# A new static order of instructions, and a new division of three kinds of work among the engines, in an attention and two-MLP kernel

## The chip, the cores and the metric

The kernel runs on one core of a Trainium2 chip. The metric is the device time of one execution, in microseconds (us), less is better. A core has a matrix engine (PE), a vector engine (DVE), an activation engine (ACT), a general engine (POOL) and a queue that issues the DMAs (SP). Each engine takes its instructions strictly in the order in which the program lists them, and waits where an instruction needs something that another engine has not finished. So the order of each list is a part of the program, and it is this order that the change makes anew.

## The reference, cut to what matters

Attention (2 batches, 8 heads, 768 positions, head size 64; a query sees 8 global keys and 96 local ones), then a first MLP with a rational activation, then a second one with a softmax gate and a layer norm.

```python
a = np.exp(scores - max); a = a / (sum + 1e-9); x = a @ v       # attention, masked
h = x @ w_in                                                     # 1536 x 512 @ 512 x 2048
P = a[0] + a[1]*h + a[2]*h**2 + a[3]*h**3
Q = 1.0 + abs(b[0])*abs(h) + abs(b[1])*h**2
g = P / (Q + 1e-6)
x = g @ w_out                                                    # 1536 x 2048 @ 2048 x 512
h = x @ w_in2; sm = softmax(h); solu = h * sm
ln = (solu - mu) / sqrt(var + 1e-6) * g_ln
out = ln @ w_out2
```

## The kernel before

**Words.** Matmul operands are kept as two words: a high one, which the matrix engine's rounded 32-bit type can hold, and a low one, the rest. Each product is three matmul passes: high by high, high by low, low by high. The weights come in as 64-bit numbers, and DVE makes 32-bit ones of each 128x512 piece in three steps (L705, L709, L713), 48 times; a copy then makes the high word (on the engine that the string WHX names) and a subtraction the low word (`minus`, L149, on POOL, or on DVE for the pieces listed in WDVE).

**Stages.** Tokens go in four blocks of 384. For a block, 12 attention units (one token tile of 128 by one pair of heads) fill x: scores on PE (L568, L571), masked maximum on DVE (L577), exponential on ACT (L585), transposes on PE (L601), their copy out by ACT or DVE (L619, chosen by TRX), the product with v on PE (L608, L614). After four units a tile is normalized on DVE (L637), transposed (L641) and split in two words. Then come the steps of the first MLP, 64 in all: block 0 with the first 8 of the 16 pieces of the hidden size, blocks 1, 2 and 3 with all 16, block 0 with the last 8 (its x was stored and is loaded again). A step is: 12 matmuls for h (L797, L799 for the high word of x, L803 for the low one); an elementwise chain for g; 9 matmuls of g with w_out (L890, L891, and L896 for the low word of g). From about 403 us on, a second phase handles the second MLP in 12 token tiles; there PE has nearly all the work (L977 to L979, L1062 to L1064).

**The elementwise chain of a step** reads h from a PSUM bank: two activations (ACT, L826 and L828), a product (DVE, L829), a square (DVE as L836 or ACT as L832, chosen by the string SQX, one letter a step), logarithm and exponential (ACT, L840, L841), three products (DVE: L842, L844, L846). L846 is the last; its result is g. EPX chooses where the chain's middle value lives: an SBUF tile ("t") or a PSUM bank. Then the high word of g is a copy (ACT, DVE or POOL, by GHX), and the low word is a subtraction, in the kernel before always on POOL (L149).

**What sets the order.** The program first records some 2,100 operations, each with its engine, a duration in a model and what it needs. A list scheduler (class `Plan`) then walks through model time and writes each engine's list: among the operations that can start, it takes the one whose due time, less a lead by kind (LEADS), is earliest. UW, WS and M2 say at which step the attention units of later blocks, the second half of the first MLP's weights, and the weights of the second MLP are recorded. Where the plan has a gap on PE of over 0.7 us, it puts small matmuls of the identity there (L389, "fill"). DVE instructions marked `lock` are those whose operands all lie in SBUF; the plan lets them wait for a POOL instruction that runs, and the other way round. SP's list holds all loads in the order of the plan. Nothing is decided while the kernel runs.

Of the kernel before, what the change touches and what calls it, by code (L numbers as in the profile page):

```python
# [35 lines left out]
UW = {1: (1, 4), 2: (8, 15), 3: (25, 9)}  # L36
# [9 lines left out]
WLEAD = 33.8  # L46
# [147 lines left out]
class Plan:  # L194
# [5 lines left out]
    SEM, PORT, PORT2 = 0.04, 0.02, 0.05  # L200
# [7 lines left out]
    def op(self, eng, lat, fn, r=(), w=(), new=(), occ=None, lock=False, lead=0.0, move=0.0, after=(), tag=""):  # L208
        o = Op()
        o.i, o.eng, o.lat, o.fn, o.lock, o.lead, o.move, o.tag = len(self.ops), eng, lat, fn, lock, lead + LEADS.get(tag, 0.0), move, tag  # L210
        o.occ = occ if occ is not None else lat - 0.1 if eng in ("ACT", "DVE") else lat
        if lock:
            o.lat, o.occ = o.lat + WAIT, o.occ + WAIT
# [44 lines left out]
    def late(self, d, o):  # L258
        return self.SEM + (0.05 if o.eng == "POOL" else 0.0) + (0.1 if d.eng == "POOL" and o.eng == "PE" else 0.0)
# [15 lines left out]
    def run(self, emit=True, fill=None):  # L275
# [14 lines left out]
        def add(o):  # L290
            o.t0 = max((d.end + self.late(d, o) for d in o.deps if d.eng != o.eng or o.eng in ("SP", "X")), default=0.0)
            ready[o.eng].append(o)
# [5 lines left out]
        while left:  # L298
# [53 lines left out]
            if o.lock:  # L352
                port = o.end - (self.PORT2 if e == "POOL" else self.PORT)
# [1078 lines left out]
```

## Time and profile before

| | us |
|---|---|
| median of 3 executions (lowest, highest) | 551.47 (551.41, 552.12) |
| the profiled execution | 551.61 |
| its span, first to last instruction | 549.8 |
| PE busy in the span | 525.0 (95%) |
| DVE busy | 469.3 (85%) |
| ACT busy | 319.9 (58%) |
| POOL busy | 138.3 (25%) |

The span and the profiled execution differ by 1.8 us, which lie outside the first and last instruction. Busy time of PE is from a record's start to its modelled end, and matmuls overlap: two that follow each other closely both count as running. How much work PE has is therefore read from the distance between the starts of matmuls in a stretch without a wait.

### The profile page before, as it was taken

To read this page: it belongs to the slowest core of one execution; us is meant where nothing else is said; L and a number is where in the kernel's file an instruction comes from. 1 tells how busy PE (TensorE), PEld (TensorE's weight loads), DVE (VectorE), ACT (ScalarE), POOL (GpSimd) and SP (SyncE) were. 2 spreads that over 40 slices of the span, in tenths; PEclk is the share of its full clock that TensorE was granted. 3 is DMA by queue.
4 is the path that set the end of the run, shared out by engine and by line. 5 is a ranking of instruction groups with operands and counts; after the bars stand their busy time and mean duration, and the time that the engine had idled before them with its cause. 6 is when DMAs were issued, how large, how long until landed. Compare 5 with 4: busy or idle time off the path is not lost.

```text
span 549.8 us, 9337 instructions
## 1 busy us (share of the span) xinstructions
PE 525.0 (95%) x3224; PEld 434.3 (79%) x3224; DVE 469.3 (85%) x1046; ACT 319.9 (58%) x733; POOL 138.3 (25%) x144
## 2 busy tenths in 40 slices
PE   7899897999999999999999999998999999999995
PEld 5577676887787877778988789887778888888885
DVE  6867898999999999879889999999978988788760
ACT  6559485987786765765868545547234443344330
POOL 1301142342441322113235435344530000000000
PEclk9899898999999999999999999999999999999998
DMA  7688664356446323530024511024166688747601
GB/s 239 182 265 312 178 207 126 112 156 202 147 156 203 111 67 101 179 135 1 0 78 138 202 62 40 4 93 153 39 221 222 222 272 262 255 163 257 232 38 44
DMA packets 34326, 83.53 MB, mean 152 GB/s; under 512 B 4192, under 2 KB 11616, under 8 KB 34272
## 3 DMA queue, kind: packets, MB, share of 16 engines
q1 hardware_dynamic: 34272, 82.86, 46.6%
q8 instruction: 27, 0.44, 0.3%
q14 instruction: 27, 0.22, 0.1%
HBM read 74.98 MB, written 7.86 MB: 151 GB/s over the span
## 4 chain that ended last, share of the span: by engine, by line
PE 56%; DVE 30%; ACT 9%; issue 3%; DMA 0%; ACTq 0%; DVEq 0%
PE pb L1062 4%; PE pb L1064 4%; DVE t L842 4%; PE pb L1063 4%; PE pb L979 4%; PE pb L977 4%; PE pb L978 4%; PE pb L797 4%; PE pb L614 4%; PE pb L799 4%; PE pb L803 3%; DVE t L846 3%; DVE t L836 3%; DVE pb L844 3%; DVE cv L709 3%
## 5 line engine op out<-in xcount | busy, mean ns | idle before, releaser
L149 POOL TENSOR_TENSOR g<-t,g 128x384 fp32r<-128x384 f32 x64 | 71.2, 1114 | 139.8 <-PE pb L896 47.0
L797 PE MATMUL pb<-x,w 128*128 128x384 f32 x256 | 89.6, 350 | 3.1 <-DVE t L829 2.4
L799 PE MATMUL pb<-x,w 128*128 128x384 f32 x256 | 87.4, 342 | 0.0
L890 PE MATMUL pb<-w,g 128*128 128x512 f32 x192 | 77.7, 405 | 1.8 <-DVE y L920 1.8
L891 PE MATMUL pb<-w,g 128*128 128x512 f32 x192 | 75.5, 393 | 0.0
L149 POOL TENSOR_TENSOR w<-wst,w 128x512 fp32r<-128x512 f32 x31 | 41.7, 1347 | 79.0 <-ACT w L669 42.7
L803 PE MATMUL pb<-x,w 128*128 128x384 f32 x256 | 57.9, 348 | 0.0
L826 ACT ACTIVATE t<-pb,poly 128x384 f32<-128x384 f32 x64 | 42.8, 668 | 25.1 <-PE pb L803 16.2
L896 PE MATMUL pb<-w,g 128*128 128x512 f32 x192 | 56.8, 404 | 0.0
L797 PEld LDWEIGHTS pb<-x,w 128*128 128x128 f32 x256 | 48.8, 191 | 8.4 <-DVE t L829 5.7
L799 PEld LDWEIGHTS pb<-x,w 128*128 128x128 f32 x256 | 48.9, 191 | 1.5
L585 ACT ACTIVATE e<-e,st 128x192 f32<-128x192 f32 (+1 forms) x96 | 41.9, 439 | 13.9 <-DVE st L577 13.7
L803 PEld LDWEIGHTS pb<-x,w 128*128 128x128 f32 x256 | 45.2, 190 | 5.4 <-issue 1.7
L890 PEld LDWEIGHTS pb<-w,g 128*128 128x128 f32 x192 | 36.0, 188 | 10.6 <-DVE y L920 2.7
L713 DVE SCALAR_TENSOR_TENSOR wst<-wst,cv 128x512 int32<-128x512 int32 x48 | 41.6, 868 | 1.0
L829 DVE SCALAR_TENSOR_TENSOR t<-t,poly,pb 128x384 f32<-128x384 f32 x64 | 38.7, 606 | 3.8 <-ACT t L828 3.4
L828 ACT ACTIVATE t<-pb,poly 128x384 f32<-128x384 f32 x64 | 36.9, 577 | 7.8 <-DVE t L844 4.4
L891 PEld LDWEIGHTS pb<-w,g 128*128 128x128 f32 x192 | 36.1, 188 | 5.8
L709 DVE SCALAR_TENSOR_TENSOR cv<-wst,cv 128x512 int32<-128x512 int32 x48 | 39.2, 817 | 1.5
L1062 PE MATMUL pb<-w,lh 128*128 128x512 f32 (+1 forms) x104 | 40.1, 386 | 0.0
L1064 PE MATMUL pb<-w,ll 128*128 128x512 f32 (+1 forms) x104 | 39.1, 376 | 0.0
L896 PEld LDWEIGHTS pb<-w,g 128*128 128x128 f32 x192 | 34.0, 188 | 6.0 <-issue 2.2
(173 smaller groups left out, 1143.6 us busy)
## 6 DMA issues: line engine op xcount, KB each, us to landing
wst<-in_w_in SPq DMA_DIRECT2D x24, 512.0 KB, 4.0
wst<-in_w_out SPq DMA_DIRECT2D x24, 512.0 KB, 3.9
t<-in_w_in SPq DMA_DIRECT2D x24, 512.0 KB, 4.3
t<-in_w_out SPq DMA_DIRECT2D x24, 512.0 KB, 4.1
v<-in_qkv SPq DMA_DIRECT2D x40, 256.0 KB, 3.0
qk<-in_qkv SPq DMA_DIRECT2D x40, 192.0 KB, 2.8
y_d<-y SPq DMA_DIRECT2D x12, 256.0 KB, 3.3
y<-y_d SPq DMA_DIRECT2D x12, 256.0 KB, 3.2
```

Of the source, the lines that this page charges most:

```text
L149: eng.tensor_tensor(out=out, in0=a, in1=hi.bitcast(F32), op=ALU.subtract)
L585: act.activation(out=x, in_=x, func=AF.Exp, scale=-1.0, bias=st[:, 0, c:c + 1], accum_out=st[:, 1, c:c + 1])
L709: dve.scalar_tensor_tensor(out=o, in0=w1, scalar=-0x40000000, in1=o, op0=ALU.bitwise_and, op1=ALU.bitwise_or)
L797: pe.matmul(out=pb[:, g.h.slot, 0:n], lhsT=wt[wh.slot][:, cs[p]], rhs=xt[x[0].slot][:, p, 0:n], start=(p == 0), stop=False)
L799: pe.matmul(out=pb[:, g.h.slot, 0:n], lhsT=wt[wl.slot][:, cs[p]], rhs=xt[x[0].slot][:, p, 0:n], start=False, stop=False)
L803: pe.matmul(out=pb[:, g.h.slot, 0:n], lhsT=wt[wh.slot][:, cs[p]], rhs=xt[x[1].slot][:, p, 0:n], start=False, stop=(p == 3))
L826: op("ACT", 0.2 + 0.46 * k, lambda: act.activation(out=T(g.c), in_=h(), func=AF.Square, scale=poly[:, 0:1], bias=poly[:, 1:2]), r=[g.h, vp ...
L890: pe.matmul(out=pb[:, y[i].slot, :], lhsT=gt[g.gh.slot][:, c], rhs=wt[wh.slot], start=g.first, stop=False)
L891: pe.matmul(out=pb[:, y[i].slot, :], lhsT=gt[g.gh.slot][:, c], rhs=wt[wl.slot], start=False, stop=False)
L896: pe.matmul(out=pb[:, y[i].slot, :], lhsT=gt[g.gl.slot][:, c], rhs=wt[wh.slot], start=False, stop=g.last)
L1062: pe.matmul(out=pb[:, b.slot, c], lhsT=lh[:, f, :], rhs=wh[:, c], start=(f == 0), stop=False)
L1064: pe.matmul(out=pb[:, b.slot, c], lhsT=ll[:, f, :], rhs=wh[:, c], start=False, stop=(f == 7))
```

## The change

The engine of three kinds of work is chosen anew, letter by letter: squares on DVE 13 of 64 (before 32), the rest on ACT; low words of g on DVE 29 of 64 (before none), the rest on POOL, by a new string GLX; the middle value of the chain in SBUF for 26 steps (before 16). Smaller: high words of g, ACT 28, DVE 16, POOL 20 (before 33, 15, 16); high words of weights, ACT 24, DVE 11, POOL 13 (before 28, 7, 13); low words of weights on DVE 18 (before 17); copies of transposes on DVE 15 of 48 (before 10). The durations and release delays in the plan's model are replaced by others, the leads by kind are new, and a table NUDGE adds a lead to nearly every single operation. The weights of the second half and the later blocks' attention are recorded at other steps. What is computed stays the same, and so does the number of matmuls, apart from the fills: 28 rows of them in PE's list, before 43 (a row is two matmul records in the trace).

```diff
-UW = {1: (1, 4), 2: (8, 15), 3: (25, 9)}
+UW = {1: (2, 4), 2: (5, 11), 3: (11, 15)}
-WS = (1, 24)
-M2 = (29, 35)
+WS = (6, 2)
+M2 = (26, 25)
-SQX = 'AAADAAAAAAAAAAAAAAAAAAAADDDDDDDDDDDDAAAADDAAAAADDDDDDDDDDDDDDDDD'
-EPX = 'ttpspptsppsssssspppptpppttssttttptppppttppssppppstpspppspssstsst'
-GHX = 'AAAAAAAAAADPAAAAPDDADDADDDAAPADPPAPDDAAADAAAPPPDDPPPADPPPAAAAAAP'
+SQX = 'AAAAAAAAAAAAAAAAAAAADAAADAAAAAADAADADAAADAAAAAAAADDDADADDAAAAAAD'
+EPX = 'ttttppssssssstsppsssssssssppsptstttttsstpttssttttttpttpppptspttt'
+GHX = 'PAAAAAPPDPADDAPPAPPAAAAPDAAAAADDPPAPPDDPPDPDAADDPDAAAAAAAPDPDADP'
+GLX = 'PPPPPPPPPPPPPDDPPDPPDPPDPPPPDDDDPPDDPPDPPPDDDDPPDDDPDDPDPDDDDDDD'
+NUDGE = {1130: -29.6, 650: 41.5, 791: -1.6, 825: -23.3, 1201: -26.6,
...
-    SEM, PORT, PORT2 = 0.04, 0.02, 0.05
+    SEM, PORT, OWN = 0.036, 0.135, 0.033
...
     def late(self, d, o):
-        return self.SEM + (0.05 if o.eng == "POOL" else 0.0) + (0.1 if d.eng == "POOL" and o.eng == "PE" else 0.0)
+        if d.eng == o.eng and o.eng in ("PE", "ACT", "DVE", "POOL"):
+            return self.OWN if o.eng in ("ACT", "DVE") else -1e3
+        return self.SEM + {"POOL": 0.041, "PE": 0.017}.get(o.eng, 0.0) - o.adv
...
-        op("PE", 1.39 * k + 0.3, hi, r=[wh, wl, x[0]], new=[g.h], occ=1.39 * k, tag="h")
+        op("PE", 1.39 * k + 0.165, hi, r=[wh, wl, x[0]], new=[g.h], occ=1.39 * k, tag="h")
...
-        gl.append(op("POOL", 0.12 + 0.94 * k, lambda: minus(nc, pool, gt[g.gl.slot][:, 0:n], T(g.c), gt[g.gh.slot][:, 0:n]),
-           r=[g.c, g.gh], new=[g.gl], lock=True, tag="gl"))
+        x = GLX[len(gs)]
+        gl.append(op("POOL" if x == "P" else "DVE", 0.12 + 0.89 * k if x == "P" else 0.15 + 0.4 * k,
+                     lambda: minus(nc, pool if x == "P" else dve, gt[g.gl.slot][:, 0:n], T(g.c), gt[g.gh.slot][:, 0:n]),
+                     r=[g.c, g.gh], new=[g.gl], lock=True, tag="gl" if x == "P" else "glD"))
```

What this does to the lists, at three places. In the rows that follow, names are those of the program (pb is PSUM, w a word of a weight, wst the staged weight, cv the conversion's middle value, e and pt the softmax, v the values, xq a normalized tile, g a word of g), and lines of the changed kernel are 2 to 12 higher than those of the one before (L389 is L392, L846 is L856, L890 is L902).

PE, just ahead of the first matmuls of a g with w_out, before:

```order
L614 MATMUL pb<-v_185,pt_190 64x64 x2
L601 MATMUL pb<-ident,e_188 128x128 x3
L389 MATMUL pb<-ident 128x128 x5
L614 MATMUL pb<-v_186,pt_190 64x64 x2
L614 MATMUL pb<-v_186,pt_190 64x128 x2
L614 MATMUL pb<-v_186,pt_190 64x64 x2
L389 MATMUL pb<-ident 128x128 x4
L641 MATMUL pb<-ident,xq 128x128 x4
L890 MATMUL pb<-w_95,g_157 128x512
```

and now:

```order
L807 MATMUL pb<-x_161,w_93 128x384
L809 MATMUL pb<-x_161,w_94 128x384
L813 MATMUL pb<-x_162,w_93 128x384 x4
L611 MATMUL pb<-ident,e_189 128x128 x3
L902 MATMUL pb<-w_95,g_157 128x512
L903 MATMUL pb<-w_96,g_157 128x512
```

There were two groups of fills between attention work; now the h of the fourth step and a transpose stand there. Up to the 22nd step's first L890, PE's list had 37 rows of fills and 36 attention units; now 22 and 33.

DVE, between the third and the fourth step's L846 (now L856), before:

```order
L846 SCALAR_TENSOR_TENSOR t<-t,poly,pb 128x384
L713 SCALAR_TENSOR_TENSOR wst_153<-wst_153,cv 128x512
L844 SCALAR_TENSOR_TENSOR pb<-t,pb 128x384
L846 SCALAR_TENSOR_TENSOR t<-t,poly,pb 128x384
L149 TENSOR_TENSOR w_100<-wst_153,w_99 128x512
```

and now:

```order
L839 SCALAR_TENSOR_TENSOR t<-t,poly,pb 128x384
L647 TENSOR_TENSOR xq<-pb,st_193 128x512
L723 SCALAR_TENSOR_TENSOR wst_154<-wst_154,cv 128x512
L681 CAST w_109<-wst_154 128x512
L715 TENSOR_SCALAR cv<-wst_151 128x512
L839 SCALAR_TENSOR_TENSOR t<-t,poly,pb 128x384
L151 TENSOR_TENSOR x_164<-pb,x_163 128x4x128
L719 SCALAR_TENSOR_TENSOR cv<-wst_151,cv 128x512
L852 SCALAR_TENSOR_TENSOR t<-t,poly,pb 128x384
L723 SCALAR_TENSOR_TENSOR wst_151<-wst_151,cv 128x512
L854 SCALAR_TENSOR_TENSOR t<-t 128x384
L856 SCALAR_TENSOR_TENSOR t<-t,poly 128x384
```

Conversions of weights and attention work have moved ahead of the early steps' last products. Ahead of the fourth L846, DVE had done 7 conversions and 19 units' maxima; now 13 and 24. Ahead of the 22nd it had done 28 conversions and 36 units; now 31 and 36, and besides 4 low words of g, 2 low and 4 high words of weights, 2 copies and 2 products L829 more.

DVE late in the first phase, about the 58th step, before:

```order
L713 SCALAR_TENSOR_TENSOR wst_152<-wst_152,cv 128x512
L842 SCALAR_TENSOR_TENSOR t<-t,pb 128x384
L844 SCALAR_TENSOR_TENSOR pb<-t,pb 128x384
L846 SCALAR_TENSOR_TENSOR t<-t,poly,pb 128x384
L836 SCALAR_TENSOR_TENSOR t<-t,poly 128x384
L671 CAST g_159<-t 128x384
L829 SCALAR_TENSOR_TENSOR t<-t,poly,pb 128x384
L149 TENSOR_TENSOR w_99<-wst_152,w_100 128x512
```

and now:

```order
L719 SCALAR_TENSOR_TENSOR cv<-wst_154,cv 128x512
L852 SCALAR_TENSOR_TENSOR t<-t,pb 128x384
L854 SCALAR_TENSOR_TENSOR pb<-t,pb 128x384
L856 SCALAR_TENSOR_TENSOR t<-t,poly,pb 128x384
L151 TENSOR_TENSOR g_160<-t,g_159 128x384
L852 SCALAR_TENSOR_TENSOR t<-t,poly 128x384
L854 SCALAR_TENSOR_TENSOR t<-t 128x384
L856 SCALAR_TENSOR_TENSOR t<-t,poly 128x384
```

The square L836 is gone from DVE here and a low word of g (L151) has come. Behind the 22nd step DVE's list has 12 squares (before 31), 25 low words of g (before none) and 2 conversions fewer.

## Rows read from the trace of the kernel before

**Rows 1.** Stretch, length, busy PE, PEld, DVE, ACT, POOL (instructions), clock, DMA share, GB/s.

```profile
0.00:20.00 20.00, 15.37 (x87) 11.89 (x88) 12.38 (x58) 10.28 (x34) 3.95 (x13) 0.92 0.71 228
20.00:100.00 80.00, 73.03 (x660) 55.89 (x659) 65.95 (x176) 55.32 (x153) 18.56 (x18) 0.96 0.66 208
100.00:184.70 84.70, 82.90 (x544) 68.13 (x543) 80.96 (x176) 67.83 (x159) 31.87 (x29) 1.00 0.53 168
184.70:280.00 95.30, 95.11 (x657) 78.63 (x656) 85.00 (x186) 63.47 (x147) 22.91 (x23) 1.00 0.23 72
280.00:403.00 123.00, 117.78 (x567) 101.17 (x565) 114.57 (x182) 68.24 (x131) 57.72 (x59) 1.00 0.31 96
403.00:550.00 147.00, 140.81 (x714) 118.55 (x714) 110.43 (x273) 54.81 (x113) 3.34 (x4) 0.99 0.59 200
sum 550.00, PE 525.00 PEld 434.27 DVE 469.29 ACT 319.94 POOL 138.34; mean PE 87.50 PEld 72.38 DVE 78.21 ACT 53.32 POOL 23.06
```

**Rows 2.** PE in order of time: start, duration, line, [idle before]; three places.

```profile
199.48 0.56 PE L571 MATMUL pb<-qk 64*64 64x192 f32 x8
199.96 0.67 PE L614 MATMUL pb<-v,pt 128*64 128x64 f32 x12
200.56 0.50 PE L890 MATMUL pb<-w,g 128*128 128x512 f32 x1
...
233.83 0.49 PE L601 MATMUL pb<-ident,e 128*128 128x128 f32 x3
234.15 0.60 PE L641 MATMUL pb<-ident,xq 128*128 128x128 f32 x4
...
279.29 0.40 PE L890 MATMUL pb<-w,g 128*128 128x512 f32 x1
...
283.49 0.40 PE L890 MATMUL pb<-w,g 128*128 128x512 f32 x1
```

**Rows 3.** The chain that ended last, in the second phase: start, duration, what.

```profile
444.91 0.87 PE pb L1040 x8
...
457.19 0.88 PE pb L1040 x8
```

**Rows 4.** DVE in order of time: the 22nd L846 and the next record.

```profile
184.11 0.61 DVE L846 SCALAR_TENSOR_TENSOR t<-t,poly,pb 128x384 f32<-128x384 f32 x1
184.64 0.42 DVE L705 TENSOR_SCALAR cv<-wst 128x512 int32<-128x512 int32 x1
```

**Rows 5.** DVE groups by line and shape: count, busy us, mean ns, idle before.

```profile
L713 DVE SCALAR_TENSOR_TENSOR wst<-wst,cv 128x512 int32<-128x512 int32 x48 | 41.6, 868 | 1.0
L709 DVE SCALAR_TENSOR_TENSOR cv<-wst,cv 128x512 int32<-128x512 int32 x48 | 39.2, 817 | 1.5
L829 DVE SCALAR_TENSOR_TENSOR t<-t,poly,pb 128x384 f32<-128x384 f32 x64 | 38.7, 606 | 3.8 <-ACT t L828 3.4 <-ACT t L826 0.2
L836 DVE SCALAR_TENSOR_TENSOR t<-t,poly 128x384 f32<-128x384 f32 x32 | 27.1, 846 | 2.3 <-ACT t L828 2.2
L844 DVE SCALAR_TENSOR_TENSOR pb<-t,pb 128x384 f32<-128x384 f32 x48 | 26.8, 558 | 1.0
L705 DVE TENSOR_SCALAR cv<-wst 128x512 int32<-128x512 int32 x48 | 24.9, 519 | 0.1
L149 DVE TENSOR_TENSOR w<-wst,w 128x512 fp32r<-128x512 f32 x17 | 13.0, 769 | 0.2
L844 DVE SCALAR_TENSOR_TENSOR t<-t 128x384 f32<-128x384 f32 x16 | 11.6, 726 | 0.2
```

**Rows 6.** POOL's and ACT's groups, and PE's fills, in the same form.

```profile
L149 POOL TENSOR_TENSOR g<-t,g 128x384 fp32r<-128x384 f32 x64 | 71.2, 1114 | 139.8 <-PE pb L896 47.0 <-ACT g L669 41.1 <-DVE g L671 11.6
L832 ACT ACTIVATE t<-t,poly 128x384 f32<-128x384 f32 x32 | 19.8, 618 | 3.1 <-DVE pb L844 1.7
L389 PE MATMUL pb<-ident 128*128 128x128 f32 x86 | 15.2, 325 | 1.7 <-POOL ident masks.py:199 1.7
```

**Rows 7.** Who waited for whom: line, released by: us in total, times, longest.

```profile
ACT pb L840 <- DVE t L836: 26.6, 14, 3.8
```

More of the change, by code (lines that the diff above doesn't have):

```diff
@@ L206, in __init__, with op @@
         self.ops, self.pe = [], 0.0
-    def op(self, eng, lat, fn, r=(), w=(), new=(), occ=None, lock=False, lead=0.0, move=0.0, after=(), tag=""):
+    def op(self, eng, lat, fn, r=(), w=(), new=(), occ=None, lock=False, lead=0.0, move=0.0, after=(), tag="", adv=0.0):
         o = Op()
[L210 to L213, printed above, removed]
+        o.i, o.eng, o.lat, o.fn, o.lock, o.lead, o.move, o.tag = len(self.ops), eng, lat, fn, lock, lead + LEADS.get(tag, 0.0) + NUDGE.get(len(self.ops), 0.0), move, tag
+        o.occ = occ if occ is not None else lat - {"ACT": 0.1, "DVE": 0.082, "POOL": 0.03}.get(eng, 0.0)
+        o.adv = adv
         o.new, o.due, o.end = list(new), None, None
@@ L290, in add @@
         def add(o):
[L291 removed]
+            o.t0 = max([0.0] + [d.end + self.late(d, o) for d in o.deps])
             ready[o.eng].append(o)
@@ L352, in run @@
             if o.lock:
-                port = o.end - (self.PORT2 if e == "POOL" else self.PORT)
+                port = o.end
             if e == "SP":
@@ L765, in seen @@
                 dve.scalar_tensor_tensor(out=a, in0=w1, scalar=0x40000000, in1=a, op0=ALU.bitwise_xor, op1=ALU.bitwise_and)
-        op("SP", 2.0, lambda: sync.dma_start(out=words(), in_=src.bitcast(I32)), occ=0.42, new=[st], move=2.0, after=gl[-4:] + joins[-1:], tag="ckl")
-        op("DVE", 0.7, seen, r=[st], **{"new" if first else "w": [vacc]}, tag="ck")
+        op("SP", 2.0, lambda: sync.dma_start(out=words(), in_=src.bitcast(I32)), occ=0.43, new=[st], move=1.4, after=gl[-4:] + joins[-1:], tag="ckl")
+        op("DVE", 0.682, seen, r=[st], **{"new" if first else "w": [vacc]}, tag="ck")
     def w_verdict():
@@ L835, in e_ops @@
         else:
-            op("DVE", 0.2 + 0.43 * k, lambda: stt_(out=T(g.a), in0=T(g.b), scalar=poly[:, 5:6], in1=T(g.b), op0=ALU.add, op1=ALU.mult),
+            op("DVE", 0.2 + 0.412 * k, lambda: stt_(out=T(g.a), in0=T(g.b), scalar=poly[:, 5:6], in1=T(g.b), op0=ALU.add, op1=ALU.mult),
                r=[g.b], new=[g.a], lock=True, tag="q")
@@ L981, in p2_h @@
         for half in range(2):
-            o.op = op("PE", 3.06, lambda half=half: mm(half), r=[o.yh, o.yl] + [v for m in range(4) for v in W["i2", m, half]],
+            o.op = op("PE", 2.885, lambda half=half: mm(half), r=[o.yh, o.yl] + [v for m in range(4) for v in W["i2", m, half]],
                new=[o.h[half]] if half else [o.h[0]], occ=2.73, tag="h2")
```

159 lines of the change are left out of this document (82 added, 77 removed).

## The prediction

> **What bounds the kernel now.** I read the busy times by stretch first [rows 1], because an average over the span hides that the stages differ. From 403 us on PE has the work: a token tile of the second phase takes 457.19 - 444.91 = 12.28 us in the chain that ended last [rows 3], PE is busy without a gap but for the ends, and twelve tiles are 147 us, which no order can shorten. From 100 to 403 us PE has 2, 0 and 5 us without a running matmul, and DVE is busy 81 of 85, 85 of 95 and 115 of 123 us. So both are near full there, and an order can win little. In the first 100 us it is otherwise: PE stands for 11.6 us, DVE for 7.6 + 14.0 = 21.7 us, and the granted clock is 0.92 and 0.96, that is, at times the lower of its two levels (1.2 instead of 2.4 GHz).
>
> The busy share of PE (95%) says too little, since overlapped matmuls count from start to modelled end. So I price PE's work by distances of starts where nothing waits [rows 2]. A step of the first MLP without attention: 283.49 - 279.29 = 4.20 us. An attention unit: 0.48 (L571, 199.48 to 199.96) + 0.60 (L614, to 200.56) + 0.32 (L601, 233.83 to 234.15) = 1.40 us. I then take one milestone, the 22nd step, since there the two engines can be compared: DVE finishes its L846 at 184.11 + 0.61 = 184.7 us [rows 4], but PE begins the first L890 of that step only at 200.6 us [rows 2]. PE is 15.9 us behind DVE. Up to there PE's list holds 21 whole steps, 6 more h of 2.1 us each and 36 units: 88.2 + 12.6 + 50.4 = 151 us of work in 200.6 us, so about 49 us are lost. Behind it lie 549.8 - 200.6 = 349.2 us with 37 x 4.20 + 6 x 2.1 + 12 x 1.40 + 147.4 = 332 us of work, and only 17 us are lost. The time to win lies ahead of the 22nd step.
>
> **The engines' loads.** They alone promise nothing. 29 low words of g leave POOL (29 x 1.114 = 32 us, [rows 6]) and come to DVE. The trace has no such instruction on DVE; the nearest rows are L844 of the same 384 columns, 0.558 us where an operand is in PSUM and 0.726 where all lie in SBUF [rows 5]. I take 0.65: 29 x 0.65 = 19 us more. 19 squares leave DVE: 19 x 0.846 = 16 us less [rows 5], and cost ACT 19 x 0.618 = 11.7 us [rows 6]; ACT hides that, being busy 68 of 123 us between 280 and 403 us [rows 1]. If that cover were gone, it would cost 11.7 us at most. The hand-over from DVE to ACT behind a square is saved with it; ACT waited 26.6 us in 14 such waits [rows 7], mostly with work to spare. Copies, casts and one low word add about 6 us to DVE (11 instructions of at most 0.77, [rows 5]), so DVE has some 9 us more in all, and POOL some 31 less. On totals alone the change is neutral or a small loss for DVE; what it may win comes from where the work stands.
>
> **The first stretch, to the 22nd step.** Ahead of its L846 DVE now has 3 more conversions of 0.519 + 0.817 + 0.868 = 2.20 us, 2 more low words of weights (0.769), 4 low words of g (0.65), 2 more L829 (0.606) and 6 more casts and copies (about 0.56 by the nearest L844) [rows 5]: 6.6 + 1.5 + 2.6 + 1.2 + 3.4 = 15.3 us. Neighbouring records overlap by about 0.08 us (L846 ends at 184.72, the next record starts at 184.64 [rows 4]), 23 times, so about 13 us net. DVE's busy time to there was 12.38 + 65.95 + 80.96 = 159.3 us, its idle time 25.4 us [rows 1]. If the extra 13 us fall into that idle time, the 22nd L846 ends at 184.7 us as before; if none do, at 197.7. I take the first, because 14.0 of the 25.4 idle microseconds lie between 20 and 100 us, and the new list puts its extra work exactly there: 24 units and 13 conversions ahead of the fourth L846, where 19 and 7 stood.
>
> What changes is PE. Its list has 3 units (4.2 us) less and 22 instead of 37 rows of fills ahead of that step. 30 matmul records of 15.2 / 86 = 0.18 us [rows 6] are 5.3 us. It can follow DVE more closely: I put its first L890 of the step 3 us behind L846 (an estimate: one cast of g, of about L832's 0.6 us, and two or three groups like those of 0.5 to 0.6 us that stand ahead of it in rows 2). That is 187.7 us instead of 200.6. PE would then have lost 187.7 - 147 = 41 us instead of 49, of which the fills are 5.3; the rest must come from the 13.4 us in which it stood [rows 1].
>
> **The rest.** PE has 349.2 + 4.2 (the three units) us left, less what goes of its stalls. It stands 0.2 + 5.2 us between 184.7 and 403 us [rows 1]. There DVE loses 19 x 0.846 + 2 x 2.20 = 20.5 us and gains 25 x 0.65 = 16 us of low words and a few small ones, and POOL, which kept DVE's SBUF-only instructions waiting, has 25 instructions less. I let 3 us of the 5.4 go, with 0 and 6 as ends.
>
> **Sum.** 187.7 + 349.2 + 4.2 - 3 = 538.1 us of span, and 1.8 us outside it, as in the profiled execution (551.61 against 549.8): 539.9, about **540 us**. The profiled execution is 0.1 us from the median, so no correction is made. Low end: DVE 5 us earlier at the 22nd step, and 6 us of stalls gone, 532. High end: none of the 13 us hidden and no stall gone, 556.
>
> **Rival 1: the words moved to DVE wait for POOL.** The trace shows that DVE instructions with all operands in SBUF are stretched and others are not: 0.726 against 0.558 us for L844, 0.846 for the square against 0.606 for L829, which reads PSUM [rows 5]. The change makes 29 low words and 10 x 3 = 30 products of that kind and takes 19 squares away: 40 more. At 0.17 us each that is 7 us, most of it behind the 22nd step, where DVE is nearly full. Against it: POOL, which they wait for, runs 31 us less. With 3 us of stalls gone turned into 3 to 5 us more, the time is 546 to 548. The Trainium skill (SBUF — State Buffer, section "Who interferes with whom") says that a DVE instruction with two SBUF inputs conflicts with a POOL instruction that reads SBUF, and that whichever issues first holds the port for its whole length. By that rule the moved subtraction stays in the conflict on its new engine; the stretched rows agree, and so do the unstretched ones with PSUM operands.
>
> **Rival 2: no difference.** Some two thirds of the 13 us end up on the path (193 us for the 22nd L846), and nothing goes from the stalls: 193 + 3 + 353.4 + 1.8 = 551.
>
> **Rival 3: slower, since DVE's early list is too full.** DVE takes its list strictly in order. Between the third and fourth L846 now stand two conversions, a normalization and other work, and 6 more conversions (13 us) and 5 more units stand ahead of the fourth. A conversion in front of a product holds back that step's g, and PE behind it. If DVE still waits for scores and exponentials as before, the 25.4 us of idle time remain and the extra work adds to them. It decides from the point where less than a third of the 13 us is hidden; with none hidden the time is 197.7 + 3 + 353.4 + 1.8 = 556. For it: 7.6 of the idle microseconds are start-up, and an order fitted to one trace may meet other releases. Against it: PE's 15.9 us behind DVE are a reserve that has to be used up first.
>
> **How the numbers follow.** Forecast, 532 to 546 us: 0.58. Rival 1, 546 to 550: 0.15. Rival 2: 0.08. Rival 3, above 552.6: 0.19. A measurement here can tell about 0.2%, 1.1 us, from no change. That gives faster 0.73, same 0.08, slower 0.19. The range is 530 to 554; what is left out is the far half of rival 3 and the case that much more idle time goes than I see.
>
> **What would show it.** Right: the 22nd L846 (L856 in the new code) ends within 180 to 188 us, PE's first L890 of that step (L902) starts 2 to 6 us behind, DVE is busy over 71 of 80 us from 20 to 100 us, and about 350 us lie behind the milestone. Wrong: DVE's idle time in the first 185 us stays near 25 us (rival 3 or 2); squares, conversions and the L844 form without PSUM above their old means, with the low word of g on DVE well over 0.73 us (rival 1); PE still 10 us or more behind DVE at the 22nd step, which would mean that PE's own list and not DVE's work sets the early time; or the second phase no longer at 12.28 us a tile.

## The result, and the profile after

The changed kernel takes 531.67 us (median of four executions, 530.0 to 533.82) against 551.56 (551.41 to 552.12). The ratio is 0.964, interval 0.960 to 0.968: 19.9 us are gone, where 11.5 were forecast. The execution with the profile took 531.36 us, its span is 529.5.

| | before | after |
|---|---|---|
| span, us | 549.8 | 529.5 |
| PE, DVE, ACT, POOL busy, us | 525.0, 469.3, 319.9, 138.3 | 512.5, 453.4, 323.9, 109.9 |
| end of the 22nd step's last product on DVE (L846, now L856) | 184.7 | 176.8 |
| PE's first matmul of that step's g with w_out (L890, now L902) | 200.6 | 179.0 |
| from there to the end of the span | 349.2 | 350.5 |

By stretch, the kernel after (start and end, length, busy PE, PEld, DVE, ACT, POOL, granted clock, DMA share, GB/s), to be laid beside [rows 1]:

```profile
0.00:20.00 20.00, 17.21 (x127) 13.22 (x127) 15.36 (x77) 12.41 (x45) 2.19 (x12) 1.00 0.76 259
20.00:100.00 80.00, 78.19 (x689) 61.48 (x690) 73.74 (x203) 65.86 (x179) 25.69 (x24) 1.00 0.71 236
100.00:184.70 84.70, 83.26 (x539) 69.27 (x538) 80.71 (x170) 60.40 (x131) 33.15 (x33) 1.00 0.44 141
184.70:280.00 95.30, 95.30 (x653) 79.05 (x652) 78.44 (x175) 68.51 (x157) 20.30 (x21) 1.00 0.29 90
280.00:385.00 105.00, 104.09 (x514) 91.32 (x513) 100.66 (x185) 64.54 (x121) 28.33 (x29) 1.00 0.32 106
385.00:530.00 145.00, 134.48 (x682) 113.03 (x680) 104.46 (x262) 52.17 (x110) 0.20 (x1) 0.99 0.56 192
```

In the first 100 us PE now stands for 4.6 us (before 11.6), DVE for 10.9 (21.7), and the view gives the clock as 1.00 (0.92 and 0.96). That is not the full speed from the start: the trace's record of the clock begins with a rise to the full level, at 10.6 us (before at 6.7), and what lies ahead of the first entry counts as 1.00 in the view (see the last section). What differs is that the clock falls to the lower level three times in the first 100 us before, at 16.9, 64.7 and 88.6 us, and not once after until 526 us. The place where the forecast measured, first DVE in order of time (start, duration, engine, line), as [rows 4] before:

```profile
176.21 0.61 DVE L856 SCALAR_TENSOR_TENSOR t<-t,poly,pb 128x384 f32<-128x384 f32 x1
176.74 0.61 DVE L846 SCALAR_TENSOR_TENSOR t<-t,poly 128x384 f32<-128x384 f32 x1
```

And PE in the same form, as [rows 2] before:

```profile
178.30 0.86 PE L908 MATMUL pb<-w,g 128*128 128x512 f32 x3
179.00 0.39 PE L902 MATMUL pb<-w,g 128*128 128x512 f32 x1
```

PE was 15.8 us behind DVE there; it is 2.2 us behind now. But that is the distance at one step, and of all 64 steps it is the one at which the distance in the changed kernel is least. Other steps, read from the same traces in the same way (us):

| step | 4 | 8 | 16 | 22 | 28 | 32 | 44 | 56 | 64 |
|---|---|---|---|---|---|---|---|---|---|
| before: PE's first L890 | 92.2 | 117.7 | 166.4 | 200.6 | 238.7 | 261.8 | 314.4 | 367.6 | 400.3 |
| behind DVE's L846 | 27.0 | 13.2 | 22.6 | 15.8 | 19.6 | 22.5 | 17.9 | 18.4 | 13.7 |
| after: PE's first L902 | 82.5 | 101.4 | 151.6 | 179.0 | 219.1 | 241.0 | 291.0 | 346.4 | 376.2 |
| behind DVE's L856 | 3.4 | 7.6 | 20.0 | 2.2 | 24.8 | 26.8 | 9.4 | 10.9 | 10.1 |

Over all steps the median distance is 17.9 us before and 11.5 after. What lasts is that PE starts earlier: by 10 us at the 4th step, 16 at the 8th, 18 to 24 from the 22nd on. DVE's and POOL's groups after (count, busy us, mean ns, idle before), as [rows 5, 6] before (L709, L713, L705 are L719, L723, L715; L836 is L846; L844 is L854):

```profile
L719 DVE SCALAR_TENSOR_TENSOR cv<-wst,cv 128x512 int32<-128x512 int32 x48 | 35.6, 742 | 1.1
L723 DVE SCALAR_TENSOR_TENSOR wst<-wst,cv 128x512 int32<-128x512 int32 x48 | 33.3, 694 | 0.6
L715 DVE TENSOR_SCALAR cv<-wst 128x512 int32<-128x512 int32 x48 | 24.6, 512 | 0.7 <-DMA wst<-in_w_out 0.5
L151 DVE TENSOR_TENSOR g<-t,g 128x384 fp32r<-128x384 f32 x29 | 18.3, 633 | 0.8 <-ACT e L595 0.4
L854 DVE SCALAR_TENSOR_TENSOR t<-t 128x384 f32<-128x384 f32 x26 | 14.8, 569 | 0.3
L846 DVE SCALAR_TENSOR_TENSOR t<-t,poly 128x384 f32<-128x384 f32 x13 | 8.6, 669 | 6.1 <-ACT t L838 5.8
...
L151 POOL TENSOR_TENSOR g<-t,g 128x384 fp32r<-128x384 f32 x35 | 38.8, 1110 | 76.2 <-ACT g L679 26.8 <-PE pb L908 24.6 <-DVE g L681 11.3
```

Most forms that have all operands in SBUF became cheaper (a cast of a weight's word did not, 424 to 519 ns): the conversions 2.20 to 1.95 us apiece, L844's form 726 to 569 ns, the square 846 to 669. The low word of g on DVE takes 633 ns (0.65 was assumed). PE's longest waits after (line, released by: us in total, times, longest):

```profile
PE pb L1052 <- DVE st L1015: 3.1, 1, 3.1
...
PE pb L902 <- ACT g L679: 0.7, 1, 0.7
```

The first is new, near the end, and has an experiment of its own below.

### The profile page after: what moved, and what is told of

The parts are those of the page before. It is cut to its first block, busy times and chain, and to the rows that moved or that the text cites. A ratio compares the mean times of both kernels' runs of the same rounds, so it can differ in the third digit from the quotient of the medians.

```text
span 529.5 us, 9263 instructions
## 1 busy us (share of the span) xinstructions
PE 512.5 (97%) x3194; PEld 427.4 (81%) x3194; DVE 453.4 (86%) x1067; ACT 323.9 (61%) x738; POOL 109.9 (21%) x118
## 4 chain that ended last, share of the span: by engine, by line
PE 63%; DVE 24%; DMA 7%; ACT 2%; issue 2%; POOL 0%; SPq 0%; DVEq 0%; ACTq 0%
PE pb L807 7%; PE pb L813 7%; PE pb L809 7%; PE pb L902 6%; PE pb L908 6%; PE pb L903 6%; PE pb L624 4%; DMA t<-in_w_out 3%; PE pb L611 3%; PE pb L581 3%; DVE cv L775 3%; DMA t<-in_w_in 2%; PE pb L1074 2%; DVE st L1011 2%; PE pb L1076 2%
## 5 line engine op out<-in xcount | busy, mean ns | idle before, releaser
L807 PE MATMUL pb<-x,w 128*128 128x384 f32 x256 | 88.7, 346 | 1.3 <-DVE t L839 0.6
L809 PE MATMUL pb<-x,w 128*128 128x384 f32 x256 | 86.2, 337 | 0.0
L902 PE MATMUL pb<-w,g 128*128 128x512 f32 x192 | 76.8, 400 | 0.7 <-ACT g L679 0.7
L836 ACT ACTIVATE t<-pb,poly 128x384 f32<-128x384 f32 x64 | 42.8, 668 | 39.5 <-PE pb L813 38.0
L813 PE MATMUL pb<-x,w 128*128 128x384 f32 x256 | 55.8, 343 | 0.0
L151 POOL TENSOR_TENSOR g<-t,g 128x384 fp32r<-128x384 f32 x35 | 38.8, 1110 | 76.2 <-ACT g L679 26.8
L807 PEld LDWEIGHTS pb<-x,w 128*128 128x128 f32 x256 | 48.0, 188 | 7.4 <-DVE t L839 2.6
L151 POOL TENSOR_TENSOR w<-wst,w 128x512 fp32r<-128x512 f32 x30 | 42.1, 1404 | 43.7 <-ACT w L679 33.4
L595 ACT ACTIVATE e<-e,st 128x192 f32<-128x192 f32 (+1 forms) x96 | 41.9, 438 | 12.4 <-DVE st L587 12.1
L809 PEld LDWEIGHTS pb<-x,w 128*128 128x128 f32 x256 | 48.1, 188 | 1.3 <-DVE w L151 0.3
L813 PEld LDWEIGHTS pb<-x,w 128*128 128x128 f32 x256 | 44.1, 188 | 1.2 <-issue 0.6
L902 PEld LDWEIGHTS pb<-w,g 128*128 128x128 f32 x192 | 36.0, 188 | 9.6 <-ACT g L679 1.1
L775 DVE SCALAR_TENSOR_TENSOR cv<-t,cv 128x512 int32<-128x512 int32 x47 | 32.3, 688 | 13.3 <-DMA t<-in_w_out 8.5
L1074 PE MATMUL pb<-w,lh 128*128 128x512 f32 (+1 forms) x104 | 40.1, 386 | 0.0
L1075 PE MATMUL pb<-w,lh 128*128 128x512 f32 (+1 forms) x104 | 38.8, 373 | 0.0
```

Source lines behind the costliest of these rows:

```text
L151: eng.tensor_tensor(out=out, in0=a, in1=hi.bitcast(F32), op=ALU.subtract)
L595: act.activation(out=x, in_=x, func=AF.Exp, scale=-1.0, bias=st[:, 0, c:c + 1], accum_out=st[:, 1, c:c + 1])
L775: dve.scalar_tensor_tensor(out=a, in0=w1, scalar=0x40000000, in1=a, op0=ALU.bitwise_xor, op1=ALU.bitwise_and)
L807: pe.matmul(out=pb[:, g.h.slot, 0:n], lhsT=wt[wh.slot][:, cs[p]], rhs=xt[x[0].slot][:, p, 0:n], start=(p == 0), stop=False)
L809: pe.matmul(out=pb[:, g.h.slot, 0:n], lhsT=wt[wl.slot][:, cs[p]], rhs=xt[x[0].slot][:, p, 0:n], start=False, stop=False)
L813: pe.matmul(out=pb[:, g.h.slot, 0:n], lhsT=wt[wh.slot][:, cs[p]], rhs=xt[x[1].slot][:, p, 0:n], start=False, stop=(p == 3))
```

## Experiments

Three theories stand against each other. Theory 1: the gain is the order's (work put into idle time, PE's list close behind DVE's). Theory 2: it is the division's (POOL has 28 us less, so DVE's waits for POOL go, and DVE has fewer squares). Theory 3: it is the fills' (rows that cost PE time). For each run the trace gives the same milestone, the 22nd step: where DVE ends its last product, where PE starts the first matmul of g with w_out, and what is left of the span from there (us).

| kernel | median | ratio, interval | DVE ends | PE starts | left |
|---|---|---|---|---|---|
| before | 551.56 | | 184.7 | 200.6 | 349.2 |
| after | 531.67 | 0.964, 0.960 to 0.968 | 176.8 | 179.0 | 350.5 |
| a_words_pool | 536.79 | 0.973, 0.967 to 0.978 | 180.1 | 182.4 | 351.8 |
| a_sq_dve | 538.77 | 0.973, 0.969 to 0.977 | 177.5 | 179.7 | 360.2 |
| a_old_division | 541.67 | 0.983, 0.978 to 0.988 | 175.9 | 178.3 | 361.2 |
| b_words_dve | 549.35 | 0.996, 0.993 to 0.998 | 186.6 | 202.7 | 346.5 |
| b_words_memset | 540.41 | 0.978, 0.975 to 0.982 | 182.4 | 198.2 | 341.5 |
| b_no_fill | 556.69 | 1.006, 1.003 to 1.009 | 189.9 | 205.7 | 350.0 |
| a_no_fill | 533.72 | 0.964, 0.961 to 0.967 | 181.9 | 184.1 | 351.4 |
| a_no_nudge | 541.10 | 0.983, 0.977 to 0.988 | 167.6 | 186.4 | 350.7 |
| a_no_nudge_no_fill | 548.48 | 0.990, 0.987 to 0.994 | 174.1 | 194.5 | 352.2 |
| b_dur | 549.18 | 0.992, 0.988 to 0.996 | 184.4 | 195.4 | 349.5 |
| b_uw | 552.12 | 1.000, 0.998 to 1.001 | 187.5 | 206.1 | 344.6 |
| a_verdict_late | 530.99 | 0.959, 0.956 to 0.963 | 178.4 | 180.6 | 348.7 |

Ratios are to runs of before on the same chip. The runs of before that stood beside a_sq_dve, b_no_fill, a_no_fill and a_no_nudge_no_fill had a median of 553.44 us, those beside the others 551.5 to 551.6; across this line the ratios are to be compared, not the times. Names with a_ start from the changed kernel, names with b_ from the one before.

**The division undone, in the new order.** First the words alone (a_words_pool):

```diff
-                     lambda: minus(nc, pool if x == "P" else dve, gt[g.gl.slot][:, 0:n], T(g.c), gt[g.gh.slot][:, 0:n]),
+                     lambda: minus(nc, pool, gt[g.gl.slot][:, 0:n], T(g.c), gt[g.gh.slot][:, 0:n]),
```

> The changed kernel with its lists as they are, except that all 64 low words of g run on POOL again. Theory 1: the milestone of the 22nd step stays at 177 to 182 us, since only 4 of the 29 words lie ahead of it; behind it POOL's 32 us more stretch DVE's instructions and DVE is spared 18 us of words: 531 to 537 us. Theory 2: the waits for the port come back, L719 and L723 go up from 742 and 694 to 800 ns or more, and two thirds of the gain are lost: 543 to 552 us.

It took 536.79 us, 5.1 more than the changed kernel, at the upper end of theory 1's window; the conversions L719 and L723 rose only to 772 and 714 ns. Then the squares alone (a_sq_dve), 21 of which run on DVE in ACT's place in time:

```diff
-        if k2 == "A":
+        if k2 == "A" and SQB[len(gs)] == "A":
...
+        elif k2 == "A":
+            op("ACT", 0.17 + 0.446 * k, lambda: stt_(out=T(g.a), in0=T(g.b), scalar=poly[:, 5:6], in1=T(g.b), op0=ALU.add, op1=ALU.mult),
```

> The changed kernel with its lists as they are, except that the 21 squares that ran on DVE before and run on ACT now run on DVE again, in the place in time where ACT's list has them. Theory 2 (the division counts: DVE has 21 x 0.67 = 14 us more behind the 22nd step, and ACT waits for DVE at each): the time behind PE's first matmul of the 22nd step grows by 6 to 14 us and the whole is 537 to 546 us. Theory 1 (the order; DVE has 14 us of idle time between the 22nd step and the second phase): 531 to 535 us.

538.77 us, 7.1 more by the times and about 5 by the ratios (0.973 against 0.964), at the lower end of theory 2's window (its profiled execution took 541.76, so the table's 360.2 is some 3 us too long). Both together (a_old_division, the two edits in one kernel):

> The changed kernel with its lists as they are in time, but with the two largest parts of the old division: all low words of g on POOL, and the 21 squares that were DVE's before on DVE again. Undone one at a time they cost 5 us (words) and about 6 us (squares). Theory 1 (order first): the two undone together cost 8 to 12 us, 540 to 544 us, so that the other 8 to 11 us of the gain are the order's. Theory 2 (division first): DVE is over-full behind the 22nd step, and the time is 546 to 555 us.

541.67 us, 10.0 more, as theory 1 had it: half of the gain. The milestone tells where: PE starts the 22nd step's g at 178.3 us, as early as with the new division (179.0). All the loss lies behind it. The stretch from there to the second phase in a_old_division (columns as in the table by stretch):

```profile
178.30:395.00 216.70, 208.57 (x1196) 174.18 (x1195) 192.93 (x366) 125.76 (x265) 80.44 (x77) 1.00 0.28 90
```

and the same stretch in the changed kernel:

```profile
179.00:385.00 206.00, 205.09 (x1198) 175.13 (x1197) 184.45 (x372) 137.48 (x286) 51.13 (x52) 1.00 0.30 96
```

PE stands 8.1 us there instead of 0.9, and DVE is 8.5 us busier. The loss grows late: PE's first matmul of g comes 1.2 us later than in the changed kernel at the 44th step and 10.4 later at the 64th; ten of the 21 squares and 16 of the 29 words lie from the 44th step on. So the gain has two halves in two places: the early one stays when words and squares go back, and the new division is what lets the late stretch keep it. (The smaller choices of engine and EPX are the new ones in all three runs.)

**The division alone, in the old order.** The same 29 words on DVE in the kernel before (b_words_dve):

```diff
-        gl.append(op("POOL", 0.12 + 0.94 * k, lambda: minus(nc, pool, gt[g.gl.slot][:, 0:n], T(g.c), gt[g.gh.slot][:, 0:n]),
+        x = GLX[len(gs)]
+        gl.append(op("POOL", 0.12 + 0.94 * k, lambda: minus(nc, pool if x == "P" else dve, gt[g.gl.slot][:, 0:n], T(g.c), gt[g.gh.slot][:, 0:n]),
```

> The kernel before with its lists unchanged, except that the 29 low words of g that the change gives to DVE run on DVE in the place where POOL's list orders them in time. Theory 1 (the gain comes from the order): before's lists stay, so PE's first L890 of the 22nd step stays at 198 to 202 us (only 4 of the 29 words lie ahead of it), and the 18 us of words on DVE behind it eat what DVE's shorter waits for POOL give back: 549 to 560 us. Theory 2 (the gain comes from the division: POOL has 31 us less and DVE's waits for POOL's port go): the two conversion steps L709 and L713 fall from 817 and 868 to below 760 ns, DVE's busy time grows by less than 5 us, and the time is 538 to 546 us.

549.35 us: 2.2 us, theory 1's window. DVE's busy time fell from 469.3 to 468.1 us although it has 17.3 us of words more, so what the words cost DVE is given back by its shorter waits for POOL: theory 2's sign for the busy time came, but not its 760 ns for the conversions (762 and 794) and not its time. The milestone came 2.1 us later (202.7, where theory 1 had 198 to 202). To price those waits by themselves, POOL's reads of g were taken away; the result then lacks the low words (b_words_memset):

```diff
-        gl.append(op("POOL", 0.12 + 0.94 * k, lambda: minus(nc, pool, gt[g.gl.slot][:, 0:n], T(g.c), gt[g.gh.slot][:, 0:n]),
+        gl.append(op("POOL", 0.12 + 0.94 * k, lambda: pool.memset(gt[g.gl.slot][:, 0:n].bitcast(F32), 0.0),
```

> The kernel before with the 64 low words of g replaced by POOL memsets of zeros of the same shape, which read no SBUF (the low words of g are left out of the result this way); lists unchanged. It prices DVE's waits for the port. Theory 2: the conversions fall to about 0.42 + 0.68 + 0.68 = 1.8 us (from 2.20), DVE's busy time by 25 to 37 us, and the time to 535 to 543 us. Theory 1: DVE's busy time falls as much, but PE's first matmul of the 22nd step still comes at 195 us or later, since the order that DVE and PE keep is the old one, and the time stays above 545 us.

```profile
L713 DVE SCALAR_TENSOR_TENSOR wst<-wst,cv 128x512 int32<-128x512 int32 x48 | 35.9, 747 | 1.0
L709 DVE SCALAR_TENSOR_TENSOR cv<-wst,cv 128x512 int32<-128x512 int32 x48 | 35.7, 743 | 1.5
...
L849 POOL MEMSET g<- 128x384 f32 x64 | 27.6, 432 | 135.1 <-PE pb L896 131.3 <-DMA wst<-in_w_out 3.8
```

These groups (form as above) belong to b_words_memset: L713 was 868, L709 817 [rows 5]. The time fell by 11.1 us, which theory 2 had and theory 1 had not; but of the span's 10.0 us 7.7 lie behind the milestone and only 2.4 ahead of it, as theory 1 said of the place. The waits can be summed: over DVE's instructions with all operands in SBUF and 192 columns or more, duration less the median of the same form where no POOL instruction ran beside it (forms with three or more such instructions). That gives, ahead of DVE's milestone and behind it, 11.8 and 25.3 us before, 5.9 and 9.8 after, 7.1 and 19.4 in a_words_pool, 6.5 and 7.8 with the memsets. The Trainium skill (SBUF — State Buffer, "Who interferes with whom") says that a DVE instruction with two SBUF inputs conflicts with a POOL instruction that reads SBUF and not with one that only writes it; the run with memsets agrees, with 37.1 us of such waits down to 14.3. It agrees instruction by instruction too. Of DVE's instructions with two SBUF inputs, 24 ran there beside a memset alone, and none of them was 0.1 us over its median; 31 ran beside a POOL instruction that reads SBUF, and 19 of them were, by 10.4 us in all.

**Fills.** PE's list without them, before and after (b_no_fill, a_no_fill), one edit:

```diff
-        plan.run(True, fill)
+        plan.run(True, None)
```

> The kernel before without its 43 rows of fills (86 matmul records, 74 ahead of the 22nd step, where PE is 15.9 us behind DVE); they compute nothing. Theory 3: the fills are a good part of that delay, 74 x 0.18 = 13 us; PE's first matmul of the 22nd step comes at 187 to 193 us instead of 200.6 and the time falls to 538 to 545 us. Theory 1: what PE keeps behind DVE is the order of its attention units; the milestone comes at 196 us or later and the time is 547 to 552 us. If the clock falls for lack of them, 553 to 560 us.

> The changed kernel without its 28 rows of fills (56 matmul records of the identity, 44 of them ahead of the 22nd step); they compute nothing. Theory 3 (fills stand in PE's list where PE has work, so each row costs its own time, and a part of the gain is that there are fewer): 44 x 0.18 = 8 us less ahead of the 22nd step at most; PE's first matmul of that step comes at 171 to 176 us and the time falls to 524 to 529 us. Theory 1 (PE there waits for DVE, so that fills lie in its waits): the milestone stays within 2 us of 179.0 and the time at 529 to 533 us. If the fills keep the granted clock up, stretches at half level appear and the time rises to 533 to 540 us.

Theory 3 falls: without fills the old kernel is 3.2 us slower, and the changed one gains nothing (533.72 against 531.67, the ratio 0.964 in both; its profiled execution took 537.38). In the profiles both milestones come 5.1 us later. PE in b_no_fill, in order of time:

```profile
25.07 1.12 PE L614 MATMUL pb<-v,pt 128*64 128x64 f32 x12
26.12 0.90 PE L601 MATMUL pb<-ident,e 128*128 128x128 f32 x3
...
28.42 0.67 PE L614 MATMUL pb<-v,pt 128*64 128x64 f32 x12
...
30.42 0.55 PE L601 MATMUL pb<-ident,e 128*128 128x128 f32 x3
```

Up to some 28 us the same matmuls take 1.6 times as long as later: by these durations TensorE is at the lower of its two levels, and the first entry in this trace's record of the clock is a rise to the full one at 28.1 us. In the kernel before, fills run ahead of and between the first score matmuls, and that entry stands at 6.7 us. The fills themselves show it, 0.28 us each ahead of it and 0.15 behind:

```profile
4.89 1.65 PE L389 MATMUL pb<-ident 128*128 128x128 f32 x6
...
8.17 1.16 PE L389 MATMUL pb<-ident 128*128 128x128 f32 x8
```

So a fill stands in a wait and costs nothing, and in the kernel before it buys the full clock some 21 us sooner. That kernel has relapses too, the first at 16.9 us, behind gaps of 1.27, 0.24, 0.29 and 0.52 us (rows in order of time):

```profile
16.30 0.66 PE L608 MATMUL pb<-v,pt 128*128 128x64 f32 x4 [0.52 <-ACT pt L619]
...
17.75 1.12 PE L641 MATMUL pb<-ident,xq 128*128 128x128 f32 x4
18.79 0.92 PE L571 MATMUL pb<-qk 64*64 64x192 f32 x8
20.37 0.62 PE L571 MATMUL pb<-qk 64*64 64x192 f32 x8
```

**NUDGE.** The order by kind alone, with and without fills (a_no_nudge, a_no_nudge_no_fill):

```diff
-lead + LEADS.get(tag, 0.0) + NUDGE.get(len(self.ops), 0.0), move, tag
+lead + LEADS.get(tag, 0.0) , move, tag
```

> The changed kernel with the table NUDGE left out: the new durations, release delays, leads by kind, recording steps and the new division stay, but the single operations lose their own leads, so that the order of all lists differs. Theory 1: the time depends on the order in detail; the gain is mostly lost, 542 to 556 us, with PE's first matmul of the 22nd step at 188 us or later. Theory 2: the division of the work does it, and the order by kind suffices: 531 to 538 us.

> The changed kernel without the table NUDGE and without fills. Without NUDGE alone the time was 541.1 us; PE had 118 fill matmuls ahead of the 22nd step (44 with NUDGE), and came 18.8 us behind DVE's last product there, though DVE was 9 us earlier than with NUDGE. Theory 3: these 118 x 0.18 = 21 us are what NUDGE wins; without them PE follows DVE within 6 us, the milestone comes at 168 to 176 us, and the time is 523 to 531 us. Theory 1 (NUDGE's order itself counts): the milestone stays above 181 us and the time above 536 us.

541.10 us: NUDGE is worth 9.4 us, as theory 1 had it but for 1 us (and the milestone, 186.4, but for 1.6). DVE at the 22nd step in a_no_nudge:

```profile
167.02 0.60 DVE L856 SCALAR_TENSOR_TENSOR t<-t,poly,pb 128x384 f32<-128x384 f32 x1
```

and PE:

```profile
186.43 0.39 PE L902 MATMUL pb<-w,g 128*128 128x512 f32 x1
```

DVE reaches the 22nd step 9 us earlier than with NUDGE, since it has less other work ahead of it (busy 151.0 us to there, against 162.3). That gains nothing, because PE comes 18.8 us behind. Without fills it comes 20.4 us behind, and the kernel takes 548.48 us (by the ratios, 0.990 against 0.983, some 4 us more): the 118 fill matmuls ahead of the step were not the delay, and my reading of them as 21 us to win was wrong by its sign. Behind the milestone are left 350.7 us without NUDGE and 350.5 with it, so its whole worth lies ahead of the 22nd step.

**One part of the new order in the old kernel.** Only the model's durations and delays (b_dur: the changed kernel's plan with the old strings, leads and recording steps, NUDGE empty), and only the recording of the attention units (b_uw):

```diff
-UW = {1: (1, 4), 2: (8, 15), 3: (25, 9)}
+UW = {1: (2, 4), 2: (5, 11), 3: (11, 15)}
```

> The kernel before, with its own division of the work, its own leads by kind and recording steps, but with the plan's durations and release delays replaced by the changed kernel's, and without NUDGE: what the measured durations alone do to the order. Theory 1 in its strong form (an order from truer times is better by itself): 541 to 548 us. Otherwise (the old leads were fitted to the old durations, and an order wins only when its leads are fitted again): 550 to 565 us.

> The kernel before with one line of the change: UW, so that the attention units of the later blocks are recorded at the steps of the changed kernel (blocks 2 and 3 from steps 5 and 11 on instead of 8 and 25). If it is the earlier attention that fills PE's and DVE's idle time in the first 92 us, PE's first matmul of the 4th step's g comes at 82 to 88 us instead of 92.2 and the time is 540 to 547 us. If the rest of the order is needed for it, 549 to 560 us.

b_dur gave 549.18 us, between its two windows (its ratio, 0.992, is 547, the upper end of the first), and its executions spread from 543 to 556 us in a way that their granted clocks don't follow (543.25 at 0.996, 551.02 at 0.997); why is left open. b_uw gave 552.12: PE was 2.4 us earlier at the 4th step's g (89.8) and 5.5 later at the 22nd (206.1). Neither of these two parts alone is the gain. The leads by kind, WS, M2, EPX and the smaller choices of engine were not tried alone.

**A version that might beat both.** The changed kernel's new wait of 3.1 us has its cause on DVE, in order of time:

```profile
499.17 0.68 DVE L775 SCALAR_TENSOR_TENSOR cv<-t,cv 128x512 int32<-128x512 int32 x1
499.89 2.23 DVE L785 TENSOR_TENSOR cv<-cv 128x256 int32<-128x256 int32 x9
...
503.20 0.14 DVE L1015 TENSOR_SCALAR st<-st 128x1 f32<-128x1 f32 x1
```

L785 to L789 check the weights' range; nothing but the end of the kernel needs them. In a_verdict_late they come behind the last tile's work, by one edit:

```diff
-            op("DVE", 2.8, w_verdict, w=[vacc, vbad], tag="flag")
+            op("DVE", 2.8, w_verdict, w=[vacc, vbad], after=[fr[NTILE - 1].last], tag="flag")
```

> The changed kernel with one order edit: the check of the weights' range (L785 to L789, 9 + 3 small DVE instructions, 2.7 us at 499.9 us) comes behind the last token tile's L1015 to L1033 on DVE instead of ahead of them, where PE's L1052 waited 3.1 us for L1015. If that wait is on the path, as PE's list behind it has no other gap, the time falls by 2 to 3 us: 528 to 530 us. If the check is late next, since the end of the kernel waits for it, no change: 531 to 532 us.

DVE in a_verdict_late at the same place:

```profile
499.11 0.68 DVE L775 SCALAR_TENSOR_TENSOR cv<-t,cv 128x512 int32<-128x512 int32 x1
499.87 0.15 DVE L1015 TENSOR_SCALAR st<-st 128x1 f32<-128x1 f32 x1
...
503.05 0.15 DVE L1022 TENSOR_SCALAR st<-st 128x1 f32<-128x1 f32 x1 [0.71 <-ACT pb L1038]
504.00 0.69 DVE L151 TENSOR_TENSOR ll<-pb,lh 128x512 fp32r<-128x512 f32 x1 [0.81 <-ACT lh L1060]
```

The wait of 3.1 us is gone, and what is left behind the milestone is 348.7 instead of 350.5 us: 1.8 of the 3.1. Where the rest went is not shown. DVE's wait of 0.71 us for L1038 stands in the changed kernel too, and the one for L1060 grew from 0.32 to 0.81. The median of 530.99 us (527.93 to 532.05), between the two windows, cannot be told from the changed kernel's 531.67.

## Why the prediction was right, and where its size was off

**The sum.** Forecast: 21.6 - 8.7 = 12.9 us earlier at the milestone, 4.2 us of units later in the list, 3 us of stalls gone, in all 11.7 us of span. Measured: 21.6, and behind the milestone 350.5 us where 349.2 + 4.2 = 353.4 were due, that is 2.9 us less: 21.6 - 4.2 + 2.9 = 20.3. The whole miss of 8.7 us lies ahead of the 22nd step. So the way was right and the size was not: 531.67 us is just under the 532 to 546 that the forecast itself had, and L856's end, 176.8, is ahead of its 180 to 188.

**What the 21.6 us are.** Count each of PE's matmuls ahead of that first L890 (L902) at the median distance to the next start, by line and shape. Then the 200.6 us before are 141.3 of work, 18.1 in which the list ran fills, 13.6 in which no matmul ran and 27.6 of longer distances; the 179.0 after are 135.8, 9.6, 6.0 and 27.5. By this estimate 16.1 us are waits, filled or bare, that are gone, and 5.5 are work that now stands later (4.2 in the forecast).

**The mis-sized term: DVE's extra work there.** The forecast had +13 us busy, 172.3, and 12.4 us idle. Measured were 162.3 busy (+3.0) and 14.5 idle, which puts L856 at 176.8 instead of 184.7. The conversions hold most of it. DVE's groups of them ahead of the milestone, in the kernel before:

```profile
L713 DVE SCALAR_TENSOR_TENSOR wst<-wst,cv 128x512 int32<-128x512 int32 x28 | 23.5, 838 | 0.8
L709 DVE SCALAR_TENSOR_TENSOR cv<-wst,cv 128x512 int32<-128x512 int32 x28 | 21.6, 771 | 0.8
L705 DVE TENSOR_SCALAR cv<-wst 128x512 int32<-128x512 int32 x29 | 14.7, 505 | 0.1
```

and in the changed one:

```profile
L719 DVE SCALAR_TENSOR_TENSOR cv<-wst,cv 128x512 int32<-128x512 int32 x31 | 22.1, 714 | 0.6
L723 DVE SCALAR_TENSOR_TENSOR wst<-wst,cv 128x512 int32<-128x512 int32 x31 | 21.7, 700 | 0.5
L715 DVE TENSOR_SCALAR cv<-wst 128x512 int32<-128x512 int32 x31 | 15.4, 498 | 0.6 <-DMA wst<-in_w_out 0.5
```

Three more conversions were priced at 6.6 us. All 31 together take 59.2 us, the 28 (29 of L705) before took 59.8. The price per piece was the old list's, with its waits for POOL in it. POOL is as busy there (57.5 us, before 54.4), and the new list's conversions run beside it as often (26 of 93 instructions, before 24 of 84), but over their undisturbed medians they lose 3.6 us instead of 9.0. The other 3 us are small: casts and copies cost 2.2 us instead of 3.4, and by difference neighbours overlap by some 2 us more.

**PE 3 us behind DVE:** 2.2 measured, right for this step, from whose place in PE's list it was worked out; it does not hold for the steps around it (10.8 at the 20th, 9.6 at the 24th). The kernels with before's lists and the old recording of units are 15.8 to 16.1 us behind whether fills, POOL's reads or words are taken from them, and those with the changed lists 2.2 to 2.4: the distance at a step is written in the lists, and PE's time there moves with DVE's (2.3 us earlier both with the memsets, 5.1 later both without fills). The forecast's 5.3 us for 30 fewer fills was wrong in kind: fills ahead of the step lie in waits.

**The rest, 350.4 us forecast and 350.5 measured,** was right as a sum, and that by luck. The forecast took 3 us of stalls off the old stretch and let the second phase be. Measured from the 22nd step to the 64th (first L890, L902) are 199.7 us before and 197.2 after, though three units more (4.2 us) stand there, so that 6.7 us of stalls are gone; from there to the end are 149.5 and 153.3 us, 3.8 more, of which 3.1 are the new wait of L1052. DVE's load in that stretch counts in both orders: in the old one the memsets won 7.7 us there, with PE 15.8 us behind at the 22nd step, and in the new one the old division costs 361.2 us instead of 350.5. "On totals alone the change is neutral" was therefore wrong in the place that counts: behind the milestone, words and squares are worth 10.7 us in the new order. Why the old division fits the old order better is not shown.

**The rivals.** Rival 1 named the right resource and the wrong sign: DVE's waits for POOL fell from 37.1 to 15.8 us, although DVE has more instructions that can wait. Rival 3 did not occur: DVE's early list is fuller (73.7 of 80 us busy from 20 to 100 us, over 71 was the sign) and DVE came earlier. The second phase kept its pace: L1052 starts at 407.8 us and, six tiles later, at 481.5, 12.28 us a tile, as [rows 3].

**The clock, which the forecast left out of its sum.** In the 45 executions of the kernel before that ran beside these kernels, the time goes with the mean granted clock: 549.09 us at 0.995, 553.84 to 555.22 at 0.981 (a line through all has -3.5 us for +0.01, correlation -0.87). The changed kernel's executions at 0.997 took 531.36 and 530.0 us; the line gives 549.3 for the old one there. So some 2 us of the 19.9 may be the clock's, by this estimate; no run changed the clock alone, and the means leave out the slow start. The forecast read the 0.92 and 0.96 of the first 100 us and gave them no term; the three falls there are gone in the changed kernel, as most of PE's gaps are.

**Open:** which of the order's parts (leads, recording steps, bank choices) hold the 10 us by which a_no_nudge's milestone beats the old one, units counted. UW and the durations each alone do not. Open too: how much of the gain is DVE's shorter waits for POOL. They fell as far as with the memsets (37.1 to 15.8 and to 14.3 us), which in the old lists were worth 11.1 us; in the changed kernel order and division shorten them together.

## What to carry to other kernels

Where two engines share a path in turn, count what the one that ends last loses ahead of a milestone, waits that are filled included: here 16 us of the gain are such waits. Do not take the distance between the engines at one step for that of a stretch; it went from 2 to 27 us within ten steps. An order and a division of work can depend on each other, so each tried alone can look poor (here the words in the old order gave 2 us, the new order with the old words and squares half of the gain; the squares alone in the old order were not tried). A mean duration that contains waits belongs to the pair of lists that it was measured in: price a moved instruction by its undisturbed duration, and the waits as a term of their own.

## What the runs showed of the hardware

The granted clock in the profile does not show the slow start. This is b_no_fill by stretch (columns as above):

```profile
0.00:20.00 20.00, 10.76 (x41) 7.74 (x42) 11.90 (x57) 9.18 (x32) 3.97 (x13) 1.00 0.65 214
20.00:40.00 20.00, 18.78 (x211) 11.69 (x210) 15.54 (x61) 13.18 (x47) 3.16 (x3) 1.00 0.65 186
```

It says 1.00 while L614 takes 1.12 us at 25.07 and 0.67 at 28.42. The trace's record of the clock is not wrong there: its first entry is the rise to the full level at 28.1 us, just between the two. But the time ahead of the first entry counts as 1.00 in the mean. In every run here the first entry is such a rise, at 5.3 to 28.1 us. The durations have to be read beside the view. The Trainium skill (TensorE: Matmul & The Clock Gate, "Part 1: The HAM clock gate") says that the array starts at the lower level and that activity raises it; the durations agree.

DVE's subtraction of the same 128x384 words takes 596 ns (29 of them in b_words_dve; 551 is the median where no POOL instruction ran), POOL's 1106 to 1140, and a POOL memset of that shape 432. Beside POOL, L705, which has one SBUF input, is stretched as well: before, 415 ns where no POOL instruction ran (33 of 48), 747 where one did.
